# A ConvNeXt-V2 block: x transposed by the DMA engines, the 3x3 taps as 32x32 tiles over pixel phases, and one of three conv banks evacuated by VectorE

## The chip, the cores and the metric

The kernel runs on one core of one Trainium2 chip. The metric is the device time of one execution in microseconds, the median of three runs. Five engines work side by side: TensorE (PE in the profile; PEld is its weight load), VectorE (DVE), ScalarE (ACT), GpSimd (POOL) and SyncE (SP). In this kernel SP only issues DMAs. PSUM, which TensorE writes and VectorE and ScalarE read, is used as eight banks of 128 partitions x 512 floats.

## What is computed

```python
# x: 512 x 512 pixels, C = 96 channels, bf16; E = 4 * C = 384
out = depthwise 3x3 convolution of x with dw        # nine shifted multiply-adds
h = layernorm over the channels of each pixel (out)
h = gelu(h @ w1)                                    # 96 -> 384
gx = sqrt(sum over all pixels of h * h + 1e-6)      # one number per channel e
nx = gx / (mean over e of gx + 1e-6)
h = grn_gamma * (h * nx) + grn_beta + h
return x + h @ w2                                   # 384 -> 96
```

The sum over all pixels stands between the two matmuls: every pixel has to pass the first before any can pass the second.

## The kernel before

The image is cut into 128 blocks of four rows (GR = 4), 2048 pixels each. There are two stages.

**Stage one** runs the convolution, the layernorm and the first matmul on every block, and gathers the sums of squares. **Stage two** runs the second matmul, adds x and writes the output. The intermediate g (gelu of the first matmul) does not fit on the chip. For the blocks called "whole" (three in ten) it is stored to DRAM (`g_dram`) and read back as `gl`; five blocks are held in SBUF; for the rest only the normalised conv output is kept in DRAM (`yn_dram`), and g is made again in stage two as `gr`.

Stage one is a loop over slots, `for s in range(last_slot + 1)` (line 826). In slot s the convolution of block s runs, and beside it each later step of earlier blocks, by a table filled in advance (`put`). All engines run in program order (`InOrder`), so the order of the Python text is the order on each engine's queue.

The steps of a block that matter here:

- `load_x(s + 4)` (line 216): SP issues the load of a block into `xin`, a ring of four tiles. Each of 128 partitions holds 16 consecutive pixels and one neighbour on each side, all 96 channels in one piece of 3,456 bytes.
- `turn_x(s + 3)` (line 442): VectorE turns the tile in 32x32 squares, with two instructions (64 channels as pairs, then 32), into `xT`, a ring of five blocks. A partition of xT then holds one channel of one of the four rows.
- `conv_taps` (line 463): 72 matmuls of 64 rows by 32 columns for each block. Each reads two image rows of one group of 32 channels (64 partitions of xT) and writes one output row of the block, 32 partitions of one PSUM bank. The weights `Wq` are diagonal. The 72 come in three bursts of 24, and each burst keeps the two row halves of the array on different banks. In the usual slot the banks are 4 to 6 (`Y3`); in seven slots without MLP ("spare") they are banks 0 to 3.
- `evac` (line 496): ScalarE copies the three banks to `y_bf`, one instruction of 1536 columns (two in a spare slot).
- `stage_sq`: POOL squares y_bf into ysq. `stage_stats`: PE sums y_bf and ysq over channels with 24 small matmuls (`rowsel`). Once for a batch of four blocks, VectorE and POOL make the reciprocal standard deviation (`mom`, `var`, `nt`, `rstd`, `rt`), and it is sent through DRAM (`r_dram`) to be spread over partitions (`rbc`).
- `stage_norm`: POOL multiplies y_bf by rbc into `yn`. `stage_write` and `stage_read`: SP sends yn to DRAM in four pieces and brings it back as `ynT`, channels on partitions.
- `mlp_units` (line 699): PE multiplies ynT by w1 (`w1p`) in units of one or two banks; ScalarE applies gelu into g; VectorE takes `bn_stats` of most of g (tile `bst`), and PE makes the rest of the sums of squares as a Gram matrix. The conv bursts are laced between these units, and the order is written out by hand:

```python
conv(0)
unit(0, 2); unit(2, 1); squares(0)
conv(1, False)
...
turn_x(s + 3)
unit(3, 1); unit(4, 2); squares(1); ... unit(6, 1); squares(2); unit(7, 1)
conv(2)
evac()
... unit(8, 2); unit(10, 1); ... unit(11, 1)
```

The pixels of a row have an order of their own: pixel m * 16 + g stands at g * 32 + m. `quad` and `quad_out` (lines 116 and 119) read ynT and write PSUM so that in a quad of g the 128 columns of one group are pixels 16 apart, as the second matmul and the output need them.

Of the kernel before, what the change touches and what calls it, by code (L numbers as in the profile page):

```python
# [9 lines left out]
ACTF = mybir.ActivationFunctionType  # L10
AX = mybir.AxisListType

GR = 4
# [43 lines left out]
def kernel(  # L57
# [73 lines left out]
    consts = ctx.enter_context(tc.tile_pool(name="consts", bufs=1))  # L131
# [8 lines left out]
    w1p = consts.tile([128, E], bf16, name="w1p")  # L140
    Wq = consts.tile([128, NI, 3, GR, 32], bf16, name="Wq")
    w2_sb = consts.tile([128, NCH, C], bf16, name="w2_sb")
# [39 lines left out]
    p2 = ExitStack()  # L182
    SL = PXP + 2
    with ExitStack() as p1:
# [23 lines left out]
        Y3 = PS[:, 4:7, :]  # L208
        pc = p1.enter_context(ExitStack())
        xinpool = pc.enter_context(tc.tile_pool(name="xin", side="right", bufs=4))  # L210
        xins = {}

        def shift(h, j):
            return 1 if (h, j) == (0, GR - 1) else -1 if (h, j) == (1, 0) else 0

        def load_x(b):
            t = xinpool.tile([128, SL, C], bf16, name="xin")
            off = x.offset + b * GR * W * C
            rows = lambda p0, p1, s0, s1: (
                t[p0:p1, s0:s1, :].rearrange("p g c -> p (g c)"),  # L220
                bass.AP(x.tensor, off + (p0 * PXP - 1 + s0) * C, [[PXP * C, p1 - p0], [1, (s1 - s0) * C]]))
            if b == 0:
                pool.memset(t[0:1, 0, :], 0.0)
                parts = [(16, 128, 0, SL), (0, 16, 1, SL), (1, 16, 0, 1)]
            elif b == NBLK - 1:
                pool.memset(t[96:128, SL - 1, :], 0.0)
                parts = [(0, 112, 0, SL), (112, 128, 0, SL - 1), (112, 127, SL - 1, SL)]
            else:
                parts = [(0, 128, 0, SL)]
            for part in parts:  # L230
                o, i_ = rows(*part)
                sp.dma_start(out=o, in_=i_)
            xins[b] = t

        Wd = gpool.tile([128, NQ, NCH, QW], bf16, name="g")[:].rearrange("p t j w -> p (t j w)")[
            :, :NI * 9 * 32].rearrange("p (i k c) -> p i k c", i=NI, k=9)
        zrow = consts.tile([128, W], bf16, name="zrow")
# [7 lines left out]
        act.activation(out=Wq[:].rearrange("p i d j c -> p (i d j c)").rearrange("p (a w) -> p a w", a=3),  # L245
                       in_=zrow[:, None, :NI * GR * 32].to_broadcast([128, 3, NI * GR * 32]), func=ACTF.Identity)
        for b in range(2, min(4, NBLK)):
# [6 lines left out]
        cen = consts.tile([C, 128], bf16, name="cen")  # L254
        xtpool = pc.enter_context(tc.tile_pool(name="xt", side="right", bufs=1))
        ypool = pc.enter_context(tc.tile_pool(name="ybf", side="right", bufs=13))
# [4 lines left out]
        ynpool = pc.enter_context(tc.tile_pool(name="yn", side="right", bufs=3))  # L261
        NXT = 5
        xt_ring = []
        xt_all = xtpool.tile([128, NXT, NI, SL * MB], bf16, name="xT")
        for i in range(NXT):
            xt_ring.append(xt_all[:, i])
        assert NXT * NI * SL * MB >= NQ * NCH * QW
        g_over = xt_all[:].rearrange("p x i s -> p (x i s)")[:, :NQ * NCH * QW].rearrange(
            "p (t j w) -> p t j w", t=NQ, j=NCH)
# [129 lines left out]
        n = 0  # L399
        for h in range(2):  # L400
            for j in range(GR):
                for q in (2 * h, 2 * h + 1):
                    a = q + GR * shift(h, j) - j + 1
                    if 0 <= a < 3:
                        n += 1
                        o, i_ = Wq[32 * q:32 * q + 32, :, :, j, :], Wd[32 * q:32 * q + 32, :, 3 * a:3 * a + 3, :]
                        if n % 2:
                            act.activation(out=o, in_=i_, func=ACTF.Identity)
                        elif n % 4:
                            dve.tensor_copy(out=o, in_=i_)  # L410
                        else:
                            pool.tensor_copy(out=o, in_=i_)

        for i in range(NI):
# [35 lines left out]
        def x_rows(b, p0, p1, i, c0, n):  # L450
            t = xt_ring[b % NXT]
            if i == 2:
                return t[p0:p1, 2, c0:c0 + n]
            return t[p0:p1, 0:2, :].rearrange("p i s -> p (i s)").rearrange(
                "p (s e) -> p s e", e=2)[:, c0:c0 + n, i]

        ybf, ysq, yns, rbcs, msts, rns, rts = ({} for _ in range(7))
# [5 lines left out]
        def conv_taps(b, spare):  # L463
            if spare:
                Ua, Ub = banks(2), banks(1)
                Y = [Ua[:, 0, :], Ua[:, 1, :], Ub[:, 0, :]]
            else:
                Y = [Y3[:, i, :] for i in range(NI)]
            mms = []
            for n in range(3):  # L470
                mms.append([(h, j, (n + h) % NI, dx) for dx in (0, -1, 1) for j in range(GR) for h in range(2)])
            flat = [m for ms in mms for m in ms]
            first = {}
            last = {}
            for n, (h, j, i, dx) in enumerate(flat):
                first.setdefault((i, j), n)
                last[i, j] = n

            def burst(n, fence=True):
                k = sum(len(ms) for ms in mms[:n])  # L480
                for h, j, i, dx in mms[n]:
                    src = b + shift(h, j)
                    o0, o1 = max(0, -dx), W - max(0, dx)
                    pe.matmul(
                        Y[i][32 * j:32 * j + 32, o0:o1],
                        lhsT=Wq[64 * h:64 * h + 64, i, dx + 1, j, :],
                        rhs=x_rows(src, 64 * h, 64 * h + 64, i, MB * (1 + dx) + o0, o1 - o0)
                        if 0 <= src < NBLK else zrow[64 * h:64 * h + 64, o0:o1],
                        start=first[i, j] == k,
                        stop=last[i, j] == k,  # L490
                    )
                    k += 1
                if n < 2 and fence:
                    pe.drain()

            def evac():
                y = ypool.tile([128, NI, W], bf16, name="y_bf")
                if spare:
                    act.activation(out=y[:, 0:2, :], in_=Ua, func=ACTF.Identity)
                    act.activation(out=y[:, 2, :], in_=Ub[:, 0, :], func=ACTF.Identity)  # L500
# [320 lines left out]

        busy(FILL[1])
        turn_x(0)
        turn_x(1)
        turn_x(2)
        for s in range(last_slot + 1):
# [34 lines left out]
            elif not mlp:  # L861
                if s + 3 < NBLK:
                    turn_x(s + 3)
                for f in taps:
# [20 lines left out]
            else:  # L885
                b = mlp[0]
# [8 lines left out]
                spread_out()  # L895
                if s + 3 < NBLK:
                    turn_x(s + 3)
                unit(3, 1)
# [153 lines left out]
```

## Time and profile before

| | |
|---|---|
| median of three runs | 1479.03 us |
| lowest and highest | 1475.51, 1484.01 us |
| profiled execution: span from first to last instruction | 1480.8 us |
| HBM read, written | 273.30 MB, 156.22 MB |
| granted TensorE clock | 0.994 |

For the profiled execution the page gives the span; no time outside it is listed. "Busy" is the time in which an engine runs at least one instruction. The duration of a matmul in these views is its latency; consecutive ones overlap, so the distance between starts tells more than the durations. Conv bursts occur from 8 us to 885 us. The window views give busy microseconds of each engine in a stretch, with the instruction counts in brackets, then the granted clock, the DMA share (mean busy share of 16 DMA engines) and GB/s.

The DMA issues that belong to stage one, with their sizes:

| transfer | issues | KB each |
|---|---|---|
| xin<-in_x_dram | 126 (and 6 smaller) | 432.0 |
| yn_dram<-yn | 512 | 96.0 |
| ynT<-yn_dram | 128 | 384.0 |
| g_dram<-g | 105 | 512.0 |
| rbc<-r_dram | 124 | 128.0 |
| r_dram<-rt | 62 | 8.0 |

### The profile page before, as it was taken

Reading aid. Unit: us, or ns where it says so; the run is one execution under the profiler, and the core shown is the slowest. Engines: PE = TensorE matmul, PEld = TensorE weight load, DVE = VectorE, ACT = ScalarE, POOL = GpSimd, SP = SyncE. Lnnn points to the kernel's source line nnn. Section 1 sums busy time; section 2 is a strip of 40 time slices with the busy share of each in tenths; the row PEclk is TensorE's granted clock in tenths of the full one; section 3 lists DMA queues with packets and bytes.
Section 4 is the critical chain, followed back from the end, with each engine's and each line's share of the span. In section 5 each row is a group of like instructions: output and inputs, shape, how many; then the busy total and the mean of one; then the engine's idle time right before and its main releaser. Section 6 shows DMA issues by size and latency. Waiting matters only on the chain.

```text
span 1480.8 us, 54225 instructions
## 1 busy us (share of the span) xinstructions
PE 1391.3 (94%) x23125; PEld 810.4 (55%) x23125; DVE 1182.0 (80%) x2135; ACT 1414.4 (96%) x1595; POOL 1300.3 (88%) x922
## 2 busy tenths in 40 slices
PE   8888999999999999999999997789999999999998
PEld 3434444444444444444444445467777777776776
DVE  7849989999999999999999987965555555555555
ACT  7888989999999999999999999999999999999997
POOL 3459889998998999998999987569999999999997
PEclk9999999999999999999999999999999999999999
DMA  5568788788888888888888866669999999999997
GB/s 180 179 205 255 241 253 280 228 271 260 260 248 264 258 264 255 276 253 254 263 258 266 263 216 195 195 225 409 366 359 402 417 416 413 419 410 417 411 412 282
DMA packets 167768, 433.08 MB, mean 292 GB/s; under 512 B 31558, under 2 KB 81318, under 8 KB 163046
## 3 DMA queue, kind: packets, MB, share of 16 engines
q1 hardware_dynamic: 151284, 326.04, 66.3%
q0 software_dynamic: 14880, 103.43, 17.6%
q8 instruction: 181, 2.97, 0.8%
q14 instruction: 61, 0.50, 0.1%
q10 hardware_dynamic: 1362, 0.15, 0.1%
HBM read 273.30 MB, written 156.22 MB: 290 GB/s over the span
## 4 chain that ended last, share of the span: by engine, by line
PE 30%; ACT 24%; DMA 19%; POOL 13%; DVE 6%; issue 4%; SPq 4%; POOLq 0%; ACTq 0%; DVEq 0%
PE PS L35 30%; ACT g L35 16%; DMA out_dram<-o_sb 9%; POOL yn L35 6%; ACT y_bf L35 5%; POOL ysq L35 5%; SPq L35 4%; DMA yn_dram<-yn 3%; DVE bst L35 3%; DMA xin<-in_x_dram 2%; DMA rbc<-r_dram 2%; DMA ynT<-yn_dram 1%; DMA g_dram<-g 1%; DVE o_sb L35 1%; ACT xT L35 1%
## 5 line engine op out<-in xcount | busy, mean ns | idle before, releaser
L35 ACT ACTIVATE g<-PS 128x512 bf16<-128x512 f32 (+2 forms) x1062 | 727.7, 864 | 16.5 <-PE PS L35 15.6
L35 DVE BATCH_NORM_STATS2 bst<-g 128x6 f32<-128x512 bf16 x1110 | 671.3, 672 | 35.4 <-ACT g L35 34.5
L35 PE MATMUL PS<-ynT,w1p 128*128 128x512 bf16 x2181 | 609.6, 381 | 23.6 <-ACT g L35 5.4
L35 ACT ACTIVATE gr<-PS 128x1536 bf16<-128x1536 f32 x360 | 498.5, 1459 | 18.8 <-PE PS L35 13.8
L35 POOL TENSOR_TENSOR yn<-y_bf,rbc 128x1536 bf16<-128x1536 bf16 x126 | 391.3, 3108 | 77.3 <-ACT rbc L35 21.9
L35 DVE TENSOR_TENSOR o_sb<-PS,xb 128x384 bf16<-128x384 f32 x512 | 277.3, 556 | 227.0 <-PE PS L35 190.1
L324 POOL TENSOR_TENSOR xb<-xr,B2c 128x1536 f32<-128x1536 bf16 x118 | 368.1, 3133 | 4.3 <-DVE o_sb L35 2.0
L35 PE MATMUL PS<-xT,Wq 64*32 64x511 bf16 (+1 forms) x9198 | 340.5, 389 | 26.2 <-ACT y_bf L35 8.1
L35 POOL TENSOR_TENSOR ysq<-y_bf 128x1536 bf16<-128x1536 bf16 x114 | 313.6, 2752 | 12.8 <-ACT y_bf L35 12.8
L35 PEld LDWEIGHTS <-w1p 128*128 128x128 bf16 x2181 | 171.6, 98 | 222.0 <-issue 133.4
L35 PEld LDWEIGHTS <-gr 128*128 128x128 bf16 x4296 | 212.1, 98 | 68.9 <-issue 12.0
L35 PE MATMUL PS<-W2s,gr 128*128 128x96 bf16 x4224 | 223.5, 206 | 8.2 <-DVE o_sb L35 8.0
L35 PEld LDWEIGHTS <-Wq 64*32 64x32 bf16 x9216 | 111.9, 90 | 193.3 <-issue 145.9
L35 ACT ACTIVATE y_bf<-PS 128x1536 bf16<-128x1536 f32 (+2 forms) x135 | 199.4, 1482 | 17.4 <-PE PS L35 13.3
L35 DVE STREAM_TRANSPOSE xT<-xin 128x576 f32<-128x576 f32 (+1 forms) x256 | 181.4, 748 | 8.1 <-DMA xin<-in_x_dram 8.1
L35 PEld LDWEIGHTS <-g 128*128 128x128 bf16 x1704 | 104.9, 98 | 86.3 <-issue 54.3
L35 PE MATMUL PS<-w1p,ynT 128*128 128x256 bf16 (+2 forms) x822 | 125.8, 273 | 8.0 <-ACT xT L35 3.2
L35 PE MATMUL PS<-g 128*128 128x128 bf16 x1464 | 122.6, 220 | 2.9 <-DVE PS L35 2.6
L35 PEld LDWEIGHTS <-gl 128*128 128x128 bf16 x1680 | 82.8, 98 | 26.8 <-issue 5.0
L35 PE MATMUL PS<-W2s,gl 128*128 128x96 bf16 x1680 | 89.5, 206 | 3.4 <-DVE o_sb L35 3.2
L35 PEld LDWEIGHTS <-ynT 128*128 128x128 bf16 x822 | 64.1, 97 | 31.5 <-issue 13.7
L279 POOL DMA_DIRECT2D xr<-in_x_dram x115 | 63.7, 555 | 14.2 <-POOL xb L324 14.2
(105 smaller groups left out, 576.5 us busy)
## 6 DMA issues: line engine op xcount, KB each, us to landing
xin<-in_x_dram SPq DMA_DIRECT2D x126, 432.0 KB
g_dram<-g SPq DMA_DIRECT2D x105, 512.0 KB
gl<-g_dram POOLq DMA_DIRECT2D x35, 1536.0 KB, 11.3
yn_dram<-yn SPq DMA_DIRECT2D x512, 96.0 KB
ynT<-yn_dram SPq DMA_DIRECT2D x128, 384.0 KB
out_dram<-o_sb SPq DMA_DIRECT2D x127, 384.0 KB
xr<-in_x_dram POOLq DMA_DIRECT2D x123, 384.0 KB, 6.9
ynT<-yn_dram SPq DMA_DIRECT2D x85, 512.0 KB
```

Of the source, the lines that this page charges most:

```text
L35: r = f(*a, **k)
L279: pq.dma_start(out=xr[:], in_=x[0, r0:r0 + GR].rearrange("r w c -> (r w) c").rearrange("(p g) c -> p g c", g=PXP))
L324: pq.tensor_tensor(out=xb[:], in0=grp[q]["xr"][:], in1=bias[:, None, :].to_broadcast([128, PXP, C]), op=ALU.add)
```

## The change

Four things change together.

1. `load_x` becomes one transposing DMA for each block, issued by SP, straight into xT. The block is read as 512 rows of four neighbouring pixels (4 x 96 channels = 384 values); value c of pixel a lands at place a * 96 + c, of which 128 go on the partitions, in three layers. xT becomes a ring of six blocks. `xin`, `turn_x` and `x_rows` go.
2. The convolution works on pixel phases: a group of 32 channels of one phase lies on 32 partitions. For each of the nine taps there are twelve matmuls of 32x32, one for each phase and channel group: 108 for a block, and twelve more where a tap crosses the end of the ring. A burst holds the three dy of one dx. The diagonal weights `Wd`, which before were a step on the way to `Wq`, are used as they are.
3. PSUM then holds phase a in partitions 32a to 32a + 31, and in each row 128 columns of the block's four image rows. `evac` reorders while it copies: it reads every fourth float (`px_order`) and writes runs of 128 (`flat_order`).
4. In every slot but the spare ones VectorE copies the third bank and ScalarE the first two (1024 columns).

The channel order, `quad` and `quad_out` become plain. POOL's steps, the MLP units, the number of bn_stats and all of stage two's instructions stay as they are, but for the order in which a quad's columns are read.

```diff
     def chans(i):
-        return slice(i, 64, 2) if i < 2 else slice(64, 96)
+        return slice(32 * i, 32 * i + 32)
...
     def quad(flat_ap, t):
-        return flat_ap.rearrange("p r (t g m) -> p t g r m", t=NQ, m=MB)[:, t]
+        return flat_ap[:, :, t * 128:(t + 1) * 128]
 
     def quad_out(flat_ap):
-        return flat_ap.rearrange("p (g r m) -> p g r m", r=GR, m=MB)
+        return flat_ap.rearrange("p (a q) -> p a q", a=GR)
...
+        NXT = 6
+        W4 = W // 4
+        xt_all = xtpool.tile([128, NI, NXT * GR, W4], bf16, name="xT")
 
         def load_x(b):
-            t = xinpool.tile([128, SL, C], bf16, name="xin")
...
-                sp.dma_start(out=o, in_=i_)
-            xins[b] = t
+            s0 = b % NXT * GR
+            sp.dma_start_transpose(
+                out=xt_all[:, :, s0:s0 + GR, :].rearrange("p k r w -> p k (r w)"),
+                in_=bass.AP(x.tensor, x.offset + b * GR * W * C, [[4 * C, GR * W4], [1, 4 * C]]))
...
-        def turn_x(b):
-            xin = xins.pop(b)
-            t = xt_ring[b % NXT]
-            pairs = t[:, 0:2, :].rearrange("p i s -> p (i s)").bitcast(f32)
-            dve.transpose(out=pairs.rearrange("p (g m) -> p g m", m=MB),
-                          in_=xin[:, :, 0:64].bitcast(f32))
-            dve.transpose(out=t[:, 2, :].rearrange("p (g m) -> p g m", m=MB), in_=xin[:, :, 64:96])
...
             def burst(n, fence=True):
-                k = sum(len(ms) for ms in mms[:n])
-                for h, j, i, dx in mms[n]:
-                    src = b + shift(h, j)
-                    o0, o1 = max(0, -dx), W - max(0, dx)
-                    pe.matmul(
-                        Y[i][32 * j:32 * j + 32, o0:o1],
-                        lhsT=Wq[64 * h:64 * h + 64, i, dx + 1, j, :],
-                        rhs=x_rows(src, 64 * h, 64 * h + 64, i, MB * (1 + dx) + o0, o1 - o0)
-                        if 0 <= src < NBLK else zrow[64 * h:64 * h + 64, o0:o1],
...
+                dx = src[n][0]
+                for dy in (0, -1, 1):
+                    segs = rows_of(dy)
+                    for o0, o1, r0 in segs:
+                        for L in range(4 * NI):
+                            a, i = divmod(L, NI)
+                            a2 = a + dx
+                            w0, w1_ = (1, W4) if a2 < 0 else (0, W4 - 1) if a2 > 3 else (0, W4)
+                            v0 = w0 - 1 if a2 < 0 else w0 + 1 if a2 > 3 else w0
+                            k, r = divmod(a2 % 4 * NI + i, 4)
+                            pe.matmul(
+                                Y[i][32 * a:32 * a + 32, :].rearrange("p (r w) -> p r w", r=GR)[:, o0:o1, w0:w1_],
+                                lhsT=Wd[32 * r:32 * r + 32, i, 3 * (dy + 1) + dx + 1, :],
+                                rhs=xt_all[32 * r:32 * r + 32, k, r0:r0 + o1 - o0, v0:v0 + w1_ - w0],
+                                start=(n == 0 and dy == 0),
+                                stop=(n == 2 and dy == 1 and (o0, o1, r0) == segs[-1]),
+                            )
                 if n < 2 and fence:
                     pe.drain()
 
+            def px_order(ps):
+                return ps.rearrange("p i (q e) -> p i e q", e=NQ)
+
+            def flat_order(y):
+                return y.rearrange("p i (e q) -> p i e q", e=NQ)
...
-                    act.activation(out=y[:], in_=Y3, func=ACTF.Identity)
+                    act.activation(out=flat_order(y[:, 0:2, :]), in_=px_order(Y3[:, 0:2, :]), func=ACTF.Identity)
+                    dve.tensor_copy(out=flat_order(y[:, 2:3, :]), in_=px_order(Y3[:, 2:3, :]))
...
         for s in range(last_slot + 1):
...
             if s + 4 < NBLK:
                 load_x(s + 4)
...
-                if s + 3 < NBLK:
-                    turn_x(s + 3)
```

`rows_of(dy)`, which is new, gives the row ranges of a tap: one range where the block and its neighbour lie side by side in the ring, else two.

More of the change, by code (lines that the diff above doesn't have):

```diff
@@ L140 @@
     w1p = consts.tile([128, E], bf16, name="w1p")
-    Wq = consts.tile([128, NI, 3, GR, 32], bf16, name="Wq")
+    Wd = consts.tile([128, NI, 9, 32], bf16, name="Wd")
     w2_sb = consts.tile([128, NCH, C], bf16, name="w2_sb")
@@ L182 @@
     p2 = ExitStack()
-    SL = PXP + 2
     with ExitStack() as p1:
@@ L209 @@
         pc = p1.enter_context(ExitStack())
[L210 to L214, printed above, removed]
+        NXT = 6
+        W4 = W // 4
+        xtpool = pc.enter_context(tc.tile_pool(name="xt", side="right", bufs=1))
+        xt_all = xtpool.tile([128, NI, NXT * GR, W4], bf16, name="xT")
         def load_x(b):
-            t = xinpool.tile([128, SL, C], bf16, name="xin")
[L218 to L231, printed above, removed]
-                sp.dma_start(out=o, in_=i_)
-            xins[b] = t
-        Wd = gpool.tile([128, NQ, NCH, QW], bf16, name="g")[:].rearrange("p t j w -> p (t j w)")[
-            :, :NI * 9 * 32].rearrange("p (i k c) -> p i k c", i=NI, k=9)
+            s0 = b % NXT * GR
+            sp.dma_start_transpose(
+                out=xt_all[:, :, s0:s0 + GR, :].rearrange("p k r w -> p k (r w)"),
+                in_=bass.AP(x.tensor, x.offset + b * GR * W * C, [[4 * C, GR * W4], [1, 4 * C]]))
         zrow = consts.tile([128, W], bf16, name="zrow")
@@ L244 @@
         act.activation(out=warm[:], in_=warm[:], func=ACTF.Gelu_apprx_tanh)
-        act.activation(out=Wq[:].rearrange("p i d j c -> p (i d j c)").rearrange("p (a w) -> p a w", a=3),
-                       in_=zrow[:, None, :NI * GR * 32].to_broadcast([128, 3, NI * GR * 32]), func=ACTF.Identity)
         for b in range(2, min(4, NBLK)):
@@ L254 @@
         cen = consts.tile([C, 128], bf16, name="cen")
-        xtpool = pc.enter_context(tc.tile_pool(name="xt", side="right", bufs=1))
         ypool = pc.enter_context(tc.tile_pool(name="ybf", side="right", bufs=13))
@@ L261 @@
         ynpool = pc.enter_context(tc.tile_pool(name="yn", side="right", bufs=3))
[L262 to L268, printed above, removed]
+        assert NXT * NI * W >= NQ * NCH * QW
+        g_over = xt_all[:].rearrange("p k r w -> p (k r w)")[:, :NQ * NCH * QW].rearrange(
             "p (t j w) -> p t j w", t=NQ, j=NCH)
@@ L398 @@
                               in1=Ud[:, i, :, None].to_broadcast([128, 9, 32]), op=ALU.mult)
[L399 to L412, printed above, removed]
         for i in range(NI):
@@ L440, in setup_rest @@
             dve.tensor_copy(out=gam[:], in_=gam_bf[:])
-        def turn_x(b):
-            xin = xins.pop(b)
-            t = xt_ring[b % NXT]
-            pairs = t[:, 0:2, :].rearrange("p i s -> p (i s)").bitcast(f32)
-            dve.transpose(out=pairs.rearrange("p (g m) -> p g m", m=MB),
-                          in_=xin[:, :, 0:64].bitcast(f32))
-            dve.transpose(out=t[:, 2, :].rearrange("p (g m) -> p g m", m=MB), in_=xin[:, :, 64:96])
[L450 to L455, printed above, removed]
         ybf, ysq, yns, rbcs, msts, rns, rts = ({} for _ in range(7))
@@ L468, in conv_taps @@
                 Y = [Y3[:, i, :] for i in range(NI)]
[L469 to L477, printed above, removed]
-            def burst(n, fence=True):
-                k = sum(len(ms) for ms in mms[:n])
-                for h, j, i, dx in mms[n]:
-                    src = b + shift(h, j)
-                    o0, o1 = max(0, -dx), W - max(0, dx)
-                    pe.matmul(
-                        Y[i][32 * j:32 * j + 32, o0:o1],
-                        lhsT=Wq[64 * h:64 * h + 64, i, dx + 1, j, :],
-                        rhs=x_rows(src, 64 * h, 64 * h + 64, i, MB * (1 + dx) + o0, o1 - o0)
-                        if 0 <= src < NBLK else zrow[64 * h:64 * h + 64, o0:o1],
[L489 to L492, printed above, removed]
+            src = [(0, 0), (-1, 1), (1, 2)]
@@ new lines, in rows_of @@
+            def rows_of(dy):
+                lo, hi = max(0, -dy), GR - max(0, dy)
+                out = [(lo, hi, b, lo + dy)]
+                if dy and 0 <= b + dy < NBLK:
+                    edge = 0 if dy < 0 else GR - 1
+                    out.append((edge, edge + 1, b + dy, GR - 1 - edge))
+                if len(out) == 2 and abs(out[1][2] % NXT - b % NXT) == 1:
+                    start = b % NXT * GR + dy
+                    return [(0, GR, start)]
+                return [(o0, o1, q % NXT * GR + r0) for o0, o1, q, r0 in out]
@@ L498, in evac @@
                 if spare:
-                    act.activation(out=y[:, 0:2, :], in_=Ua, func=ACTF.Identity)
-                    act.activation(out=y[:, 2, :], in_=Ub[:, 0, :], func=ACTF.Identity)
-                else:
-                    act.activation(out=y[:], in_=Y3, func=ACTF.Identity)
+                    act.activation(out=flat_order(y[:, 0:2, :]), in_=px_order(Ua), func=ACTF.Identity)
+                    act.activation(out=flat_order(y[:, 2:3, :]), in_=px_order(Ub), func=ACTF.Identity)
+                else:
+                    act.activation(out=flat_order(y[:, 0:2, :]), in_=px_order(Y3[:, 0:2, :]), func=ACTF.Identity)
+                    dve.tensor_copy(out=flat_order(y[:, 2:3, :]), in_=px_order(Y3[:, 2:3, :]))
                 ybf[b] = y
@@ L822 @@
         busy(FILL[1])
-        turn_x(0)
-        turn_x(1)
-        turn_x(2)
         for s in range(last_slot + 1):
@@ L895 @@
                 spread_out()
-                if s + 3 < NBLK:
-                    turn_x(s + 3)
                 unit(3, 1)
```

## The prediction

> **What bounds the kernel now.** I read the page first, then a table by windows, then groups and timelines of the middle of stage one (the part with the convolution, to about 885 us; conv bursts occur only there). The page:
>
> ```profile
> span 1480.8 us, 54225 instructions
> PE 1391.3 (94%) x23125; PEld 810.4 (55%) x23125; DVE 1182.0 (80%) x2135; ACT 1414.4 (96%) x1595; POOL 1300.3 (88%) x922
> ...
> DMA  5568788788888888888888866669999999999997
> ```
>
> The shares mix two stages, so the next view is the table of windows (PE, PEld, DVE, ACT, POOL busy, clock, DMA share, GB/s):
>
> ```profile
> 400.00:600.00 200.00, 191.83 (x3494) 94.37 (x3479) 198.80 (x342) 199.05 (x284) 187.84 (x144) 1.00 0.83 260
> ...
> 1000.00:1200.00 200.00, 196.84 (x2880) 146.17 (x2877) 111.08 (x205) 194.45 (x142) 191.65 (x114) 1.00 1.00 393
> ```
>
> In stage one ScalarE and VectorE are both at 99%, POOL at 94%, PE at 96%, and the DMA engines at 0.83. The change touches only stage one; the second stage keeps its instructions, but for the order in which a matmul reads its columns. How long is a slot (one block of four rows)? ScalarE's timeline, and PE's beside it:
>
> ```profile
> 401.07 1.51 ACT L35 ACTIVATE y_bf<-PS 128x1536 bf16<-128x1536 f32 x1
> 402.40 5.87 ACT L35 ACTIVATE g<-PS 128x1024 bf16<-128x1024 f32 x9
> 408.03 1.58 ACT L35 ACTIVATE y_bf<-PS 128x1536 bf16<-128x1536 f32 x1
> ```
> ```profile
> 402.63 0.88 PE L35 MATMUL PS<-xT,Wq 64*32 64x512 bf16 x24
> 403.61 0.82 PE L35 MATMUL PS<-ynT,w1p 128*128 128x512 bf16 x3
> 404.36 0.89 PE L35 MATMUL PS<-xT,Wq 64*32 64x512 bf16 x24
> 405.18 0.86 PE L35 MATMUL PS<-ynT,w1p 128*128 128x512 bf16 x3
> ```
>
> One evacuation to the next is 6.96 us with no gap: ScalarE paces the slot. Over 200 to 800 us there are 85 evacuations, 7.09 us apart on average; 114 slots have conv and MLP together. The groups of 200 to 800 us give the other floors:
>
> ```profile
> L35 POOL TENSOR_TENSOR yn<-y_bf,rbc 128x1536 bf16<-128x1536 bf16 x84 | 261.1, 3108 | 20.8 <-DMA xin<-in_x_dram 8.2 <-DMA g_dram<-g 8.2 <-DMA rbc<-r_dram 3.0
> L35 POOL TENSOR_TENSOR ysq<-y_bf 128x1536 bf16<-128x1536 bf16 x84 | 231.0, 2751 | 0.0
> L35 DVE STREAM_TRANSPOSE xT<-xin 128x576 f32<-128x576 f32 x85 | 64.7, 761 | 0.0
> L35 DVE STREAM_TRANSPOSE xT<-xin 128x576 bf16<-128x576 bf16 x85 | 62.5, 736 | 0.0
> ```
>
> POOL: 3.11 + 2.75 and, once in four slots, the rstd chain of 13 operations, 4.5 us with its gaps, so 1.1: about 6.9 us a slot after overlaps. It is hardly behind ScalarE (7.0) and VectorE (7.0), and its 20.8 us of idle time ended with DMAs. So four engines end within 2% of each other. PE has about 0.3 us of waits in a slot, a floor near 6.75.
>
> **The change, part by part.** The sum is made against the profiled span, 1480.8 us; the views show no time around it, and it lies 1.8 above the median of 1479.0.
>
> The prices of the evacuation come from the groups by form of the whole run:
>
> ```profile
> L35 ACT ACTIVATE y_bf<-PS 128x1536 bf16<-128x1536 f32 x121 | 188.8, 1561 | 10.2 <-PE PS L35 6.0 <-DMA gam_bf<-in_grn_gamma_dram 4.2
> L35 DVE TENSOR_TENSOR o_sb<-PS,xb 128x384 bf16<-128x384 f32 x512 | 277.3, 556 | 227.0 <-PE PS L35 190.1 <-DMA out_dram<-o_sb 35.4 <-POOL xb L324 0.9
> L35 DVE TENSOR_SCALAR mom<-PS 128x128 f32<-128x128 f32 x31 | 8.5, 275 | 3.3 <-PE PS L35 3.3
> L35 ACT ACTIVATE y_bf<-PS 128x1024 bf16<-128x1024 f32 x7 | 7.2, 1022 | 7.3 <-PE PS L35 7.3
> ```
>
> *ScalarE.* 1536 columns become 1024: 1561 ns against 1022, -0.55 a slot: 7.0 to 6.45. Its reads are now four floats apart. No row here reads PSUM so; bounds are 1022 ns and twice that, and I take 1022, the same instruction's row.
>
> *VectorE.* Loses 0.76 + 0.74, gains one 128x512 copy out of PSUM. Rows: 128 columns cost 275 ns (mom), 384 cost 556 (o_sb); the line through them gives 0.70. Net -0.80: 7.0 to 6.2. The copy waits for the third burst, and behind it in VectorE's queue stand the bst of the next quads, which only the group's aggregate needs: nothing while VectorE has 0.8 us in hand. If the copy were late, the next conv would wait for bank 6.
>
> *PE.* 72 matmuls of 64x32 become 108 of 32x32 (118 where a ring edge splits a tap; the same columns). Now eight at a time give three passes a burst, 0.82 us start to next group. After, each pass has twelve tiles, no two alike, so again three passes if twelve run together. Bounds: nothing; or, if only eight run together, 4.5 passes, +0.32 a burst, +0.97 a slot. I take nothing, since today's eight start 2 to 3 ns apart. The Trainium skill, "PSUM — Partial Sum Buffer", on bank collisions, quotes that different row tiles must not use one bank at the same time; four row groups here write each bank, though in different 32-partition quadrants, which the same section measured as clean for two engines. Were the four taken one after the other, a burst would be four times as long and the slot 5.8 us longer, by that rule over 2000 us in all.
>
> *Start.* Wq's 12 small copies and the first turns go (-2 us on ScalarE), but the first conv stands behind the warm-up matmuls, which end at 8.1 us: 0.
>
> *SP.* A plain xin issue takes 430 ns; SP spends about 4.9 us of a slot. A transposing issue is bounded by that and by the 2.2 us that are free; no cost. load_x(s+4) now waits for conv(s-1) because it overwrites that ring slot; behind it on SP stand ynT, four yn writes, rbc, r_dram and g_dram, and POOL waits for rbc. Cover: SP issued xin at 409.29, and PE's last conv burst before it had ended at 407.6. If the cover went, SP would lose 1 to 2 us of its 2.2.
>
> *DMA, the term that decides.* 0.83 of 7.09 is 5.90 us a slot. In the trace's packets of 200 to 800 us, x's pieces (3,456 B, 172 ns, eight per engine and block) are 0.192 of the time, 1.36 us. The page agrees roughly: 66.3% for 326 MB gives 1.33 for 0.44 MB. After, 384 KB are scattered so that every pixel puts two bytes into each of 128 partitions. No row here transposes. Low end: as 3,072-byte rows (123 ns) it is 1.0 us. By 256-byte pieces (64 B take 11 ns, 1,024 B 56; 20 ns between) 1.9 us. High end: 64-byte pieces at 11 ns, as r_dram's transposed write makes, 384 per engine: 4.2 us. r_dram's is the only write here whose rows are cut up as these are, so I lean to the small side and take 3.0, midway between 1.9 and 4.2. Then the DMA engines need 5.90 - 1.36 + 3.0 = 7.54 us a slot, more than any engine. The second stage shows that they can be full (1.00), so the slot becomes 7.54.
>
> The Trainium skill, "DMA: Bandwidth & Descriptors", latency and other measured facts, gives 261 GB/s for a DMA transpose with a broken middle dimension, which speaks against my value. By it a block would take 1.5 us (an estimate) and the DMA would stay hidden, as in rival one; no run here shows it yet.
>
> *Sum.* (7.54 - 7.09) x 114 = +51 us; 1479 + 51 = 1530. DMA bounds: at 2.4 us the DMA need is POOL's 6.9 and nothing is lost; at 4.2 it is 8.74, +188, 1667.
>
> **Rivals.**
> 1. *Faster: the transpose is no dearer than 2.4 us.* Then ScalarE and VectorE fall away and POOL sets the slot. For: the DMA engines have 17% in hand. Against: POOL's idle time already ends with DMAs, and POOL itself gets nothing, so the gain is small whatever the others save: (7.04 - 6.92) x 114 = 14 us with the undisturbed period of 7.04, 1465. It decides below 2.4 us per block.
> 2. *The strided read of PSUM halves ScalarE's rate.* 2 x 1022 in place of 1561: 7.0 + 0.48 = 7.48, +0.39 x 114 = 44, 1523 with the DMA hidden. For: no contiguous run is left in the read; against: every evacuation here is set by columns alone.
> 3. *Twelve tiles don't run together.* With eight at a time PE's floor is 6.75 + 0.97 = 7.72, +72, 1551. Against: today's eight start together without a gap.
> 4. *No change:* the DMA need lands at 7.0 to 7.1 and eats what the engines gain.
>
> **How the numbers follow.** Forecast (DMA need above POOL's, up to 8.74): 0.45; rival one 0.25; two 0.11; three 0.06; four 0.10; a transpose over 4.2 us 0.03. Faster is rival one, 0.25; same is rival four, 0.10; slower the rest, 0.65. "Same" is within 0.5%, 7 us, about what a measurement of this kernel can tell from no change. The range reaches from rival one with the start's 2 us and a little more, 1460, to the DMA's high end, 1670; beyond lie a dearer transpose and two of these costs at once, about 1 in 10. The forecast's own range is 1490 to 1670.
>
> **What would show it.** Right: the DMA digits of stage one rise from 8 to 9, the evacuation period goes to about 7.5 us, ScalarE's and VectorE's shares fall to some 90%, and POOL's yn or PE's conv wait for DMAs. Wrong: a DMA share at or below 0.90 with POOL at 98% (rival one); y_bf 128x1024 at 2 us (two); bursts over 1 us (three); an SP issue over 2 us would put the bound on SP's queue instead. The second stage (1000 to 1480 us) should be as long as before within 3 us; if not, my reading of the change is wrong.

## The result, and the profile after

The changed kernel takes 1547.7 us (1543.4 to 1551.7), the kernel before, beside it on the same chip, 1480.7: a ratio of 1.044, with an interval of 1.041 to 1.048. The change costs 67 us. The page of the run after:

```profile
span 1544.4 us, 66344 instructions
PE 1428.2 (92%) x29245; PEld 879.6 (57%) x29245; DVE 1096.2 (71%) x1997; ACT 1372.3 (89%) x1588; POOL 1297.4 (84%) x917
...
DMA  8878999999999999999999997659999999999997
```

VectorE has lost 86 us of work and ScalarE 42, as meant, PE has 6,120 more matmuls, and the DMA digits of stage one went from 8 to 9. The window in the middle of stage one (PE, PEld, DVE, ACT and POOL busy, granted clock, DMA share, GB/s):

```profile
400.00:600.00 200.00, 182.02 (x4370) 98.96 (x4369) 165.68 (x285) 172.58 (x257) 173.64 (x132) 0.97 1.01 237
```

No engine of this row is at its limit any more: ScalarE went from 99% to 86%, VectorE to 83%, POOL to 87%. What is full is the row of DMA engines, 1.01, while they move less than before (237 GB/s against 260). SP's queue, which the row doesn't show, is nearly full as well: with the gaps of up to 0.15 us counted in, SP's instructions (waits inside them included) cover 576 of the 600 us from 200 to 800 us, where they covered 471 before. The groups by form of 200 to 800 us, with the new evacuation and those who wait:

```profile
L35 POOL TENSOR_TENSOR yn<-y_bf,rbc 128x1536 bf16<-128x1536 bf16 x79 | 244.6, 3096 | 62.0 <-DMA rbc<-r_dram 38.4 <-ACT g L35 19.8 <-DMA g_dram<-g 3.9
L35 PE MATMUL PS<-xT,Wd 32*32 32x512 bf16 x6252 | 217.0, 386 | 30.0 <-DVE y_bf L35 28.6 <-issue 0.7 <-ACT y_bf L35 0.3
L35 ACT ACTIVATE y_bf<-PS 128x1024 bf16<-128x1024 f32 x79 | 84.6, 1071 | 3.4 <-PE PS L35 3.4
L35 DVE CAST y_bf<-PS 128x512 bf16<-128x512 f32 x78 | 52.1, 668 | 0.0
```

79 blocks pass in 600 us where 85 did: 7.65 us each. But the median from one evacuation to the next is 7.10 us (7.04 before): most slots are no longer than before, and the loss sits in single slots of 8 to 11.6 us. One of them, by the timeline:

```profile
454.49 3.10 POOL L35 TENSOR_TENSOR yn<-y_bf,rbc 128x1536 bf16<-128x1536 bf16 x1 [4.21 <-DMA rbc<-r_dram]
...
464.48 0.32 POOL L35 TENSOR_TENSOR rstd<-nt,rn 128x64 bf16<-128x64 f32 x1
...
464.83 0.24 DVE L35 STREAM_TRANSPOSE rt<-rstd 128x64 bf16<-128x64 bf16 x1 [2.83 <-POOL rstd L35]
465.00 0.65 DVE L35 CAST y_bf<-PS 128x512 bf16<-128x512 f32 x1
...
465.70 1.43 PE L35 MATMUL PS<-xT,Wd 32*32 32x512 bf16 x34 [2.97 <-DVE y_bf L35]
...
468.33 1.51 ACT L35 ACTIVATE g<-PS 128x1024 bf16<-128x1024 f32 x2 [4.34 <-issue]
```

Read it from below. ScalarE stood for 4.34 us because PE had nothing for it; PE waited 2.97 us for VectorE to empty bank 6; VectorE's copy, 0.65 us long, stood in its queue behind `rt`, which waited 2.83 us for POOL's `rstd`; and POOL was late because its yn had stood 4.21 us for `rbc`, a DMA, until 454.49 us. A late transfer went once round all engines. Why `rbc` was late is on SP's queue, which held nearly no gap ahead of it:

```profile
443.17 2.50 SPq L35 DMA_TRANSPOSE xT<-in_x_dram  x1
445.84 0.45 SPq L35 DMA_DIRECT2D ynT<-yn_dram  x1
446.34 2.57 SPq L35 DMA_DIRECT2D yn_dram<-yn  x4
448.96 2.83 SPq L35 DMA_DIRECT2D rbc<-r_dram  x4
```

The last `rbc` was issued at 451.37 us and landed 2.9 us later. Of the 13 times in 200 to 800 us that yn waited over 0.5 us for `rbc`, SP had no gap of over 0.15 us for the 7 to 34 us ahead of the issue in 11. From its issue to its landing the `rbc` that ended such a wait took 2.6 to 4.2 us. In e1 below, with a plain load, SP's stretches without a gap were 5 to 7 us in seven of eight such waits, and the transfers took 2.5 to 3.8 us. So `rbc` came late more because it was issued late than because it took longer.

Where in the run the 67 us lie (63.6 in the two profiled executions) is read from ScalarE's evacuations: the 38th (ScalarE's 38th y_bf instruction in every kernel), the time from there to the last one with a conv, and the rest of the span.

```
                           38th at   38th to last   rest
before                      196.6       687.1       597.1
after                       210.0       740.3       594.1
e1  plain load              206.0       710.0       598.4
e10 plain load, ScalarE     209.3       698.0       596.0
e12 three orders            210.0       728.1       599.1
e5  before + transposition  216.6       740.9       594.5
e13 before + plain load     206.7       703.6       597.5
```

The second stage is as long as before (-3 us). Of what the first lost, 13 us lie in its first 210 us and 53 behind.

### The profile page after: what moved, and what is told of

Read it like the earlier page. It is cut to its first block, busy times and chain, and to the rows that moved or that the text cites. A ratio compares the mean times of both kernels' runs of the same rounds, so it can differ in the third digit from the quotient of the medians.

```text
span 1544.4 us, 66344 instructions
## 1 busy us (share of the span) xinstructions
PE 1428.2 (92%) x29245; PEld 879.6 (57%) x29245; DVE 1096.2 (71%) x1997; ACT 1372.3 (89%) x1588; POOL 1297.4 (84%) x917
## 5 line engine op out<-in xcount | busy, mean ns | idle before, releaser
L35 DVE BATCH_NORM_STATS2 bst<-g 128x6 f32<-128x512 bf16 x1110 | 680.1, 677 | 135.3 <-ACT g L35 133.9
L35 PE MATMUL PS<-xT,Wd 32*32 32x512 bf16 (+2 forms) x15336 | 382.4, 367 | 58.7 <-DVE y_bf L35 35.8
L35 PEld LDWEIGHTS <-Wd 32*32 32x32 bf16 x15336 | 180.8, 89 | 268.4 <-issue 220.6
L35 ACT ACTIVATE y_bf<-PS 128x1024 bf16<-128x1024 f32 (+1 forms) x135 | 139.9, 1041 | 37.2 <-PE PS L35 37.2
L35 DVE CAST y_bf<-PS 128x512 bf16<-128x512 f32 x121 | 81.0, 670 | 36.9 <-PE PS L35 36.8
```

Of the source, the lines that this page charges most:

```text
L35: r = f(*a, **k)
```

## The experiments

Theory: the DMA engines are full because transposing costs them 3 us a block. Rivals: the new conv's smaller tiles, the new waits of SP on PE, the new coupling of VectorE into PE's path, and the time that a transposing issue takes of SP's queue.

**e1: the same bytes, not transposed.** A plain DMA fills the same tile, which then holds x untransposed, so that the output is not the block's; the rest stays.

```
-            sp.dma_start_transpose(out=xt_all[...], in_=bass.AP(..., [[4 * C, GR * W4], [1, 4 * C]]))
+            sp.dma_start(out=xt_all[...], in_=bass.AP(..., [[NI * W, 128], [W, NI], [1, W]]))
```


> The changed kernel with the transposing load replaced by an ordinary DMA of the same 384 KB into the same ring slot, so xT holds x untransposed; all else as after. Theory (the transposition itself is the cost, 3.0 us of DMA time per block where a plain load takes about 1.36): the DMA need of a slot falls to 5.9 us, POOL sets the slot at 6.9 to 7.0, and the time is 1465 (1455 to 1480). Rival (the reordering evacuation, the VectorE copy or the 32x32 taps cost the time): it stays above 1525.

Measured: 1511.8 us, ratio 1.022 (1.020 to 1.024). Neither expectation held. 36 us of the 67 come back, and the DMA share of 200 to 800 us falls from 1.02 to 0.79:

```profile
200.00:800.00 600.00, 574.94 (x14018) 317.79 (x14027) 523.27 (x903) 550.95 (x819) 545.44 (x415) 0.99 0.79 246
```

SP's queue empties with it: a plain issue takes 0.59 us (median) in place of 2.06, and the queue is covered for 473 of 600 us, as before the change. So the transposition, as DMA time and as SP's time together, is half of the cost, and 32 us stay with no transposition at all. In the table above e1 gains 30 us behind the 38th evacuation and 4 before it.

**e2: the plain load in five DMAs** (32, 32, 32, 16 and 16 partitions), to see what SP's queue can bear.

> As the plain load, but issued as five DMAs of 32, 32, 32, 16 and 16 partitions, so that SP spends about 2.1 us per block on issuing, as it does on one transposing issue (median 2.06 us), with the same bytes. Theory (DMA engines, not SP's issuing): within 1% of the plain load in one piece, so 1465 to 1480. Rival (SP's queue is the bound: 4.9 + 2.1 us and the ring wait): near the changed kernel, 1530 to 1550.

Measured: 1699.5 us, ratio 1.149 (1.145 to 1.153). Both expectations missed: the five issues (0.59 us each at the median) filled SP's queue, which is covered for 596 of 600 us, and a slot took 8.92 us on average, at a DMA share of 0.68. A full SP queue sets the slot on its own, with the DMA engines far from full. The run was to part SP's share of the cost from the DMA engines', but it loads SP more than the changed kernel does, and so doesn't part them.

**e3: ScalarE copies all three banks**, in the changed kernel with its transposition.

```
-                    act.activation(out=flat_order(y[:, 0:2, :]), in_=px_order(Y3[:, 0:2, :]), func=ACTF.Identity)
-                    dve.tensor_copy(out=flat_order(y[:, 2:3, :]), in_=px_order(Y3[:, 2:3, :]))
+                    act.activation(out=flat_order(y[:]), in_=px_order(Y3), func=ACTF.Identity)
```


> The changed kernel with ScalarE copying all three banks, as before the change, in the new pixel order. Rival (VectorE's copy, held in its queue behind rt, stalls PE's next conv: 28.6 us of PE waits for the VectorE y_bf in 600 us): those waits go, 1548 - 35 = 1513 or less, though ScalarE then needs 7.0 us a slot. Theory (DMA need of 7.5 us a slot is the bound and the wait is only where it surfaces): within 1%, 1533 to 1560.

Measured: 1548.8 us, ratio 1.046 (1.044 to 1.048): nothing. PE's waits for VectorE's copy are gone, but VectorE's `rt` waits 48.7 us for `rstd` in place of 19.9. Giving ScalarE 0.5 us less work per slot, the heart of the change, brings nothing beside the transposing load.

**e4: `rt`'s turn behind the evacuation**, so that VectorE's copy doesn't stand behind it.

```
-                for k in get("turn"):
-                    stage_turn(k)
                 conv(2)
                 if evac:
                     evac()
+                for k in get("turn"):
+                    stage_turn(k)
```


> The changed kernel with the turn of rstd (rt) moved behind the evacuation in VectorE's queue, nothing else. Rival (VectorE's copy waits for rstd behind rt): PE's 28.6 us of waits in 600 us go and about 45 us in all, 1505 to 1520. Theory (DMA bound): POOL still waits for a late rbc, the time stays within 10 us of 1548.

Measured: 1542.9 us, ratio 1.043 (1.039 to 1.047): 5 us less by time and 2 by ratio, which the intervals don't tell from nothing. PE's waits for the copy fell from 28.6 to 8.0 us; waits of POOL and of `rt` took their place. The link in the chain was as read, but it mostly passed the delay on.

**e5: the kernel before, with a transposing load of half a block** into a tile that nobody reads.

```
+            sp.dma_start_transpose(
+                out=spare_xt[:], in_=bass.AP(x.tensor, off, [[4 * C, W // 2], [1, 4 * C]]))
```


> The kernel before, with one more transposing DMA for each block: half a block (256 rows of 384 values, 192 KB) into a scratch tile that nothing reads. It costs SP one issue (about 1 us by half of 2.06) and the DMA engines about 1.5 us a slot (half of 3.0). Theory one: the DMA need rises from 5.9 to 7.4 us a slot, 1480 + 0.35 x 114 = 1520 or more. Rival (a transposition costs nothing while DMA and SP have room, and the loss lies in the change's other parts): 1480 to 1487.

Measured: 1552.7 us, ratio 1.044 (1.039 to 1.049). Half a block's transposition alone costs the old kernel as much as the whole change. That left open whether it was the form or simply 197 KB more.

**e13: the same extra bytes, plain**, as the control.

```
+            sp.dma_start(
+                out=spare_xt[:].rearrange("p i w -> p (i w)"),
+                in_=bass.AP(x.tensor, off, [[NI * W // 2, 128], [1, NI * W // 2]]))
```


> Control for the kernel before with an unused half-block transposition added (ratio 1.044): the same 196,608 extra bytes a block by a plain DMA of 1536-byte rows. If it was the transposition's form that cost 65 us, this one is within 0.5% of the kernel before (1475 to 1490): its own DMA time is about 196,608 bytes at the load's rate, 0.7 us a slot on queues that were busy 5.9 of 7.09. If any extra 196,608 bytes, or one more DMA in SP's queue, did it, it is 1520 to 1550.

Measured: 1514.9 us, ratio 1.020 (1.015 to 1.026): between what the two theories expected. 200 to 800 us of e5, then of e13:

```profile
200.00:800.00 600.00, 550.86 (x9633) 261.67 (x9634) 549.99 (x937) 552.03 (x777) 522.61 (x386) 0.95 1.03 266
```
```profile
200.00:800.00 600.00, 568.24 (x10183) 275.90 (x10181) 579.93 (x990) 583.89 (x828) 546.13 (x416) 0.99 0.91 281
```

The form costs 1.044 - 1.020, 35 us (the interval of each ratio is 7 to 9 us to either side); the extra load as such, at a DMA share of 0.91 and with one more issue on SP, costs 30, 10 of them up to the 38th evacuation (the first one comes at 16.9 us in place of 12.1). It is the second measurement of the form's price, beside the 33 us (by ratios) of e1, and it comes from a kernel with the old conv. It doesn't part DMA time from SP's: an extra issue takes 1.6 us of SP in e5 and 0.7 in e13 (medians), and SP's queue is covered for 569 and 502 of 600 us. It also says that a load, with its issue, can cost while the DMA share is below 1.0.

**e6: the load last in SP's order of a slot**, behind `rbc`, `ynT`, the yn writes and `r_dram`.

> The changed kernel with SP's order within a slot changed: the spreading of rbc first, then ynT, yn, r_dram, and load_x last but for the g_dram store, so that neither the ring wait nor the transposition stands ahead of the small transfers that POOL waits for. Theory two: the wait on PE is met by then, and rbc comes earlier: 1510 to 1530. Theory one: the bytes and the packets are the same, 1535 to 1555.

Measured: 1538.1 us, ratio 1.034 (1.029 to 1.039), some 10 us less than the changed kernel, DMA share 0.97. The chain shown above begins with a late `rbc`, but POOL's waits for it hardly changed: 35.4 us in 13 waits, against 38.4 in 13. PE's waits for VectorE's copy fell from 28.6 to 18.8 us. Which of SP's transfers gained by the order isn't shown.

**e8 and e9: a ring of eight blocks in place of six**, with the transposition (e8) and with the plain load (e9), so that the load stops waiting for the conv.

```
-        NXT = 6
+        NXT = 8
```


> The changed kernel with a ring of eight blocks in xT instead of six, so that load_x(s+4) overwrites a block that PE left three slots ago and SP need not wait for the conv of the slot before (122.7 us of SP waits on PE in 200 to 800 us, against 18.8 before the change). Theory two (SP's queue is a chain of its own and this wait stands in it): about 30 us faster than the changed kernel, 1510 to 1525. Theory one (the DMA engines' 1.02 share alone): within 1% of 1548.

> The plain load in one piece (xT holds x untransposed) and the ring of eight. If the transposition and the ring wait are the whole loss, POOL's 6.9 us sets the slot: 1462 to 1475. If the 32 us that the plain load left come from the evacuation or the taps, it stays at 1505 to 1515.

Measured: e8 1546.3 us, ratio 1.039 (1.034 to 1.045); e9 1509.1 us, 1.015 (1.009 to 1.020). The waits of SP's queue in 200 to 800 us, for the changed kernel, for e8 and for e9:

```profile
SPq L35 <- PE PS L35: 122.7, 71, 3.1
```
```profile
SPq L35 <- PE PS L35: 122.1, 72, 2.8
```
```profile
SPq L35 <- PE PS L35: 32.2, 52, 1.9
```

With the plain load the larger ring takes 90 us of SP's waiting away (e1 had 121.5), and the time gains 3 us (11 by ratio, from e1's 1.022). With the transposition the listed wait is the same with either ring. So it isn't a wait that a larger ring ends: at the median the transposing issue starts 0.03 us behind SP's instruction before it, with six blocks and with eight, and PE's release falls within the 2 us of the issue itself, which the view counts as waiting. In e1 SP stood 1.26 us (median) before such a load. e8 therefore took no wait away, and says nothing on what SP's queue costs in the changed kernel.

**e10 and e11: what of the rest is VectorE's?** In e1 the long slots came about every 75 us, and so do the three aggregates of VectorE's sums. The timeline of e1:

```profile
710.15 2.76 DVE L35 BATCH_NORM_AGGREGATE mv<-bst 128x2 f32<-128x192 f32 x3
...
713.84 1.08 ACT L35 ACTIVATE y_bf<-PS 128x1024 bf16<-128x1024 f32 x1
...
716.34 0.67 DVE L35 CAST y_bf<-PS 128x512 bf16<-128x512 f32 x1
...
717.06 0.85 PE L35 MATMUL PS<-xT,Wd 32*32 32x512 bf16 x46 [1.46 <-DVE y_bf L35]
```

VectorE's copy starts 2.5 us after ScalarE's, and PE waits for it. e10 is e1 with e3's edit; e11 is e1 with the aggregates one to a slot:

```
                 if evac:
                     evac()
+                aggregate_next()
```


> The changed kernel with both edits of two earlier runs: x loaded by a plain DMA of the same size (the conv then reads x untransposed, so its values are not the reference's) and ScalarE evacuating all three conv banks. With the plain load alone about 30 us over the kernel before are left, in slots of some 10 us about every 75 us. Theory A: they are VectorE's: its evacuation of bank 6 stands in VectorE's queue behind a set of three BATCH_NORM_AGGREGATEs (2.76 us together; at 713.84 ScalarE began its two banks, at 716.34 VectorE its one, and PE waited 1.46 us for it). Then without VectorE's copy the time is 1480 to 1490 and the long slots are gone. Theory B, what is left is PE's (the conv as 108 small matmuls) or the DMA queue's: 1505 to 1515, as with the plain load alone.

> The changed kernel with the plain load (conv values not the reference's), VectorE still evacuating its bank, and the BATCH_NORM_AGGREGATEs issued one to a slot, straight behind the evacuation, in place of three together at a slot's end. Theory A (the residual is the three of them ahead of the evacuation in VectorE's queue): 1475 to 1490, the slots of 10 us gone, with the same work on every engine. Theory B (VectorE's copy costs by its time, wherever it stands, or the residual is PE's): 1505 to 1515.

Measured: e10 1507.0 us, ratio 1.014 (1.009 to 1.019); e11 1505.2 us, 1.012 (1.007 to 1.017). Both are where theory B put them. The aggregates delay the copy as shown, but the intervals overlap that of e9, which has the copy and the aggregates as they were. Against e1, which ran at another time, e10 is 5 us ahead by time and 12 by ratio; VectorE's part is no larger than that. My theory of the rest fell.

**e12: the orders that helped, together** (e4, e6, and the aggregates one to a slot), with the transposition.

> The changed kernel with its transposing DMA, and the three orders that helped or should help taken together: the aggregates one to a slot behind the evacuation, rt's turn behind the evacuation, the load last in SP's order of the slot. Sum of the single effects: 5 us for the turn, 10 for the load, and for the aggregates up to the 30 left over with the plain load, which gives 1505 to 1520. If the transposition itself sets the end, its queue full at a busy share over 1.0, what VectorE gives back is taken by the waits for rbc, and the time stays at 1530 to 1540.

Measured: 1538.4 us, ratio 1.034 (1.029 to 1.039), no better than e6 alone. Its groups show why:

```profile
L35 POOL TENSOR_TENSOR yn<-y_bf,rbc 128x1536 bf16<-128x1536 bf16 x80 | 247.7, 3096 | 51.5 <-DMA rbc<-r_dram 42.4 <-ACT g L35 9.2
L35 PE MATMUL PS<-xT,Wd 32*32 32x512 bf16 x6390 | 218.7, 382 | 3.1 <-issue 2.2 <-ACT y_bf L35 0.3
```

PE's conv no longer waits for VectorE's copy at all, and POOL waits 42.4 us for `rbc`. The transfers set the pace (DMA share 0.97, SP's queue covered for 561 of 600 us), and these orders mostly choose who waits for them. No version here beats the kernel before.

**What the rest is: a reading, not an experiment.** In e10 nothing of the transposition and nothing of VectorE's copy is left, yet it is 20 us (by its ratio) behind. Its timeline has a place where PE stops inside a run of twelve equal matmuls:

```profile
267.31 0.39 PE L35 MATMUL PS<-rowsel,y_bf 128*128 128x4 bf16 x10
...
269.50 0.19 PE L35 MATMUL PS<-rowsel,y_bf 128*128 128x4 bf16 x2 [1.80 <-issue]
```

"issue" means that the profile shows nothing PE waited for, and its operands had been there for the ten before. What does stand beside it are packets of 16,384 bytes on the instruction queue q8: 81 in 600 us before, 105 after, 111 in e10. PE's instructions (weight loads and matmuls) in the same time divided by these are 256, 255 and 256: one packet for every 256 instructions of PE. 72 matmuls a block with as many weight loads became 120 on average (6,120 more over 128 blocks: 108, or 144 where a tap crosses the end of the ring), and the packets' median distance went from 7.3 to 5.6 us. I took every gap of over 1.2 us between two weight loads and asked how many ended 1.1 to 1.6 us after such a packet's end (0.5 us of each 5 to 7 us, so about one in ten by chance):

```
          first 200 us            200 to 800 us
before    1 of 6,   2.0 us        0 of 1
after     9 of 14, 15.1 us        2 of 16,  4.0 us
e1        9 of 12, 15.2 us        2 of 9,   3.1 us
e10       5 of 8,   9.4 us        5 of 5,   7.9 us
e9        4 of 7,   7.4 us        1 of 9,   1.3 us
e13       1 of 9,   1.6 us        1 of 7,   2.1 us
```

In e10 these gaps are 17 us, against 12.7 us lost up to the 38th evacuation and 10.9 behind. In e13, which has the old conv, they are no more frequent than chance. In e9, as slow as e10, they are 9 us. They are thickest where conv follows conv with no MLP between them, from 64 to 112 us, and there the granted clock falls as well (the last three figures of a row are clock, DMA share and GB/s). After, then before:

```profile
88.00:94.00 6.00, 5.54 (x144) 2.11 (x132) 0.00 (x0) 2.99 (x3) 5.59 (x8) 0.50 0.64 135
94.00:100.00 6.00, 5.20 (x132) 1.68 (x120) 0.84 (x2) 2.51 (x2) 5.21 (x2) 0.50 0.72 178
```
```profile
88.00:94.00 6.00, 4.96 (x152) 2.55 (x146) 3.46 (x7) 4.93 (x6) 6.00 (x3) 1.00 0.73 199
94.00:100.00 6.00, 5.80 (x114) 2.68 (x98) 2.89 (x5) 5.84 (x8) 3.39 (x2) 1.00 0.66 172
```

I take part of the rest to be PE's own instructions arriving late, and the clock that follows. It agrees in place and in size for e10, less well for e9, and no run here shortened PE's instructions alone; that run would settle it. Two other candidates stand in the same traces. POOL's yn still stood idle for 32.8 us in 600 in e10 (20.8 before), 18.3 of them for `rbc` (3.0 before). And one conv burst in three, where a tap crosses the end of the ring, has 48 matmuls and takes 0.92 us where the others take 0.79, some 10 us of PE's time in 600. The Trainium skill, "Runtime: NRT & Kernel Launch", in "Instruction fetch mechanics", says that the sequencer is refilled in blocks of 256 instructions, which agrees with the packets, and that the refill is hidden behind the rate of issue, which these gaps speak against.

## Why the prediction was right, and where it wasn't

The direction holds, and so does the size within a wide range. Of the mechanism, half holds: the transposing load costs, and DMA transfers end the waits. The sum was +51, and it is +67, made of other parts: 33 to 36 us where the sum had 51, and 32 where it had nothing. That the two errors are of opposite sign and partly cancel is luck. Of the signs named ahead, the DMA digits rose from 8 to 9, POOL's yn waits for a DMA, and the second stage is as long as it was; the period is 7.65 us where 7.5 was forecast, and ScalarE and VectorE fell further than to 90%. One sign of being wrong came too: an SP issue over 2 us (2.06 at the median in 200 to 800 us).

*DMA, the term that decided.* The price per block was right: 1536 packets of 256 bytes take 0.393 of the DMA engines in 200 to 800 us, 3.0 us a slot, the value that I took. Its working was not. The pieces are neither many nor slow: 93% of the packets take 18 ns or less, which for the 96 packets of an engine and block makes 1.73 us, and of the first four blocks, with little beside them, three took 1.5 to 1.8 us from first packet to last and one 2.6. The other part is 1,179 packets (1% of them) of over 0.5 us, 39% of the transposition's time. At 461 us eighteen such packets began between 461.24 and 461.49 us and all ended between 462.86 and 462.89, while an instruction packet stood from 460.86 to 462.07: it looks as if the engines waited for each other, and time goes by in which no piece of x lands. Why isn't shown. The step from 3.0 us to a slot of 7.54 was also too simple: a slot became 7.65 against 7.31 with the plain load, 0.34 of the 0.45 us forecast, and it comes as single long slots, not as a longer period. The term is worth 33 to 36 us, not 51, and that holds the SP time of the transposing issue as well.

*The rule of the Trainium skill, "DMA: Bandwidth & Descriptors", latency and other measured facts* (261 GB/s; by it a block takes 1.5 us, an estimate): near what the first blocks show alone, half of what a block costs beside other traffic. The measurement decides, and taking 3.0 against the page was right.

*Nothing besides the DMA costs.* The step that failed, shown by e1: without the transposition the kernel is still 32 us slower than before. Where this lies is not settled. *Start: 0* failed by 6 to 13 us up to the 38th evacuation in e1, e9 and e10. *PE: cost 0* is the part that I suspect. What I weighed there was right: 36 matmuls of a burst take 0.79 us start to start (24 took 0.81), so twelve tiles run together, and rival three falls. The rule that the Trainium skill, "PSUM — Partial Sum Buffer", quotes on bank collisions, that different row tiles must not use one bank at the same time, isn't borne out for row tiles in different quadrants: by my reading of it the burst would have been four times as long. What I left out is that a block's matmuls grow by 48 on average, which are 96 more instructions to be brought in (I had 118 matmuls for a block at the ring's end; it has 144). That this makes the 20 us of e10 is my reading, not shown.

*ScalarE: -0.55, strided read free.* Right: 1071 ns (1022 unstrided), 0.90 us start to start. Rival two falls. *VectorE: 0.70 for the copy.* 668 ns. "The copy holds nothing" was wrong as a reading, since the next conv did wait for bank 6 for 28.6 us, but e3 and e12 give nothing back when that wait goes, so it had little price of its own.

*SP: no cost.* Not shown, and the traces speak against it. An issue of the transposition takes 2.0 us (median; 1.35 at least) against 0.43, which uses most of the slack up: SP's queue is covered for 576 of 600 us, and late `rbc` were issued late. e2 shows what a full SP queue can cost at a DMA share of 0.68. How much of the 33 to 36 us is SP's time and how much the DMA engines' stays open: e5 and e13 differ in both, e8 took no wait away, and no run issued the transposition from another queue, which would part them.

*Rival one* (1465) would not have come about with a cheap transposition: e1 has one, in effect, and is 32 us slower than before.

## What to carry to other kernels

Moving a shuffle from an engine to the DMA is paid in DMA time, and loads have a price before the share reaches 1.0: one plain load of 197 KB more per slot, with its issue, took it from 0.83 to 0.91 and cost 30 us. Price a transposing DMA by what it takes beside the kernel's other traffic, not alone, and by what its issue takes of the issuing queue. Before you trust a listed wait of an issuing queue, look whether the queue stood still or whether the release fell within a long issue. When matmuls are cut into smaller tiles, count PE's instructions as well as its columns.

## What the runs showed of the hardware that I had not expected

- A transposing DMA of 393,216 bytes: 1.5 to 1.8 us with little beside it (one of four: 2.6), 3.0 us of all 16 engines beside other traffic, with eighteen long packets ending together within 0.03 us; 1.35 to 3.9 us of SP's queue for its issue.
- One instruction packet of 16,384 bytes per 256 instructions of PE, and, with the new conv, gaps of 1.2 to 2.5 us between weight loads that end 1.1 to 1.6 us after such a packet (9 of 14 gaps in the first 200 us, 1 of 6 before). The cause isn't shown.
- A granted clock of 0.50 for 12 us where PE had stopped for no longer than 1.7 us at a time.
- Four row groups writing one PSUM bank in different quadrants ran together: 36 matmuls of 32x32 in 0.79 us.
